# A gated mix of a state-space convolution and a GLU on one core: table parameters prepared for four channel groups at once, sums formed in place, PSUM banks and merge weights changed

## The chip, the cores and the metric

The program runs on one core of one Trainium2 chip. The metric is the time of one execution on the device, in microseconds (us), as the median of several runs. TensorE (PE in the rows, its weight loads PEld), VectorE (DVE) and ScalarE (ACT) each run their own list of instructions in order; SyncE (SP) issues all the DMAs, in order too. GpSimd does next to nothing here.

## The reference

The input u has 2048 rows (positions) of 512 channels. Three things are computed from it in float32:

```
g = sigmoid((u * gate_w).sum(-1))                       # one number a row
# a: a state-space convolution for each channel d, 128 states n
dt = exp(log_dt);  P[d,n,l] = exp(dt * A * l)           # A = A_re + i A_im
K[d,l] = real(sum_n C[d,n] * P[d,n,l] * dt * B[d,n])
a = causal_convolution(u, K) + u * Dskip                # by FFT in the reference
# b: a gated linear unit, 512 -> 1792 -> 512
b = (sigmoid(u @ w_gate) * (u @ w_up)) @ w_down
out = g * a + (1 - g) * b
```

## The kernel before

**The GLU** is most of TensorE's work. The 2048 rows are handled in two halves of two blocks of 512 (`half`, `sb`), the 1792 hidden columns in 14 pieces of 128 (`f`). Each float32 operand is split into a rounded high part and the rest (`split`: a copy on ScalarE, a difference on VectorE), and a product is made of three matmuls. So `hidden` issues 2 x 12 matmuls of 512 columns for each (half, sb, f) into two PSUM banks named `gups` (gate and up); `post` then takes a sigmoid of the gate (`sg`, ScalarE), multiplies it into the up bank (VectorE), and splits the product into `h` (ScalarE, VectorE). `down` multiplies `h` by the down weights into a bank named `dps`: for each of 3 or 4 pieces f (`GROUPS`) and each of 4 slices of 128 rows it issues 3 matmuls per f, so that 9 or 12 matmuls make one dps group; `add` then adds the bank, times 1 - g, to the accumulator `acc` (the first group of a row tile by a copy on ScalarE, the others on VectorE). The two kinds of matmul have one form and follow one another without a change of mode.

**The convolution** works by tables and three stages of small Fourier transforms. For each of 16 groups of 32 channels, `bases` takes the parameters `prm` and dt into `pg` and `dt`, makes angles and magnitudes (`aa`, `tn`, `ex`, `ep`) with sines and exponentials on ScalarE, the weights `w` = dt B C in parts, and the multipliers `bz`; `tables` makes two tables `T` (five doublings) and `B` from them on VectorE; TensorE multiplies these in 128 small matmuls (`kps`). `first` transforms the result (`wps`) and stores it as `a_k`. `rows` and `urest` do the same for u (`ups`, stored as `a_u`) and compute the row gate g. `passes` then runs 16 steps for each of two column halves j: `s2u` and `s2k` transform, VectorE multiplies (`tt`) and combines (`y`), `ips` transforms back, and the result goes to memory (`b_s`). `finals` takes it back (`b_in`), makes the last transform (`fps`) and adds it, times g, to the accumulator: for the first eight row tiles that was stored as `acc0`, so it is read back as `al` and the sum goes through `o` to the output. `steps` makes dt itself from log_dt at the start, by some twenty very small VectorE instructions.

**The order of the work** is made at build time. Each of these functions is a strand that yields (engine, planned duration, what to issue, what it depends on). `Plan.run` takes again and again the strand whose instruction has the smallest key: its planned start, plus the strand's entry in `BIAS`, plus `CHANGE` times the price of a change of mode. Only the resulting order and the semaphores go to the chip; planned times don't. `PACE` holds back the row tiles, `EARLY` says how long ahead of its data a strand may claim a bank, `SLACK` adds to planned latencies. Buffers are `slots`, taken and freed in planned time. PSUM's eight banks are dealt out by `BANKS`: `gu` for gups, `dn` for dps, `xb` for all the small transforms.

Of the kernel before, what the change touches and what calls it, by code (L numbers as in the profile page):

```python
# [36 lines left out]
NG = 16  # L37
ANGLES = list(range(33)) + [64 << k for k in range(5)]
# [7 lines left out]
BANKS = dict(gu=3, dn=2, xb=3)  # L46


BIAS = dict(x=-0.32, w=-0.26, split=0.4, rows=-0.12, dn=0.37, urest=1.2, bases=0.15, tables=0.35, first=0.46,
            hidden=0.91, post=0.08, down=0.69, add=0.25, passes=0.18, step=0.38, finals=0.54, last=0.21, const=4.77)  # L50
CHANGE = dict(ACT=0.5, PE=0.5)

XLATE = 0
PACE = [11.7, 12.7]
SLACK = dict(dma=0, eng=0)
EARLY = 0.21
# [156 lines left out]
def body(ctx, tc, xp, xt, prm, ldt, dsk, gw, wgu, wdn, c_wu, c_wf, c_wk, c_ww, c_pw, out):  # L213
# [47 lines left out]
    def steps():  # L261
# [27 lines left out]


    BZ, WS, PG, EX, EP, TA, TB, T2, KST, KEV = (slots(kp, n, k, s) for n, k, s in (
        ("bz", 1, [P, 3, 5, 32]), ("w", 1, [P, 3, 2, 32]), ("pg", 1, [P, 6, 32]), ("ex", 1, [P, 32, 2, NA]), ("ep", 1, [P, 32, NP]),
        ("ta", 1, [P, 32, 2, 32]), ("tb", 1, [P, 32, 2, 64]), ("t2", 2, [P, 32 * NA]), ("kst", 1, [P, 8, 64]), ("kev", 1, [P, 32, 64])))
    base = [[Ev(), None] for _ in range(NG)]
    kdone = [Ev() for _ in range(NW)]
    kleft = [w // 64 for w in WIDTHS]

    def bases():

        yield E["dt"]  # L300
        yield E["pw"]
        for gi in range(NG):
            t0 = [E["dt"].t, E["pw"].t]
            pgs, = yield PG, 1
            pg = pgs.tile("pg")
            dt = kp.tile([P, 1, 32], F32, tag="dt", name="dt")
            ta = yield "SP", kb(96), lambda: S.dma_start(pg, prm[gi].rearrange("p (a b) -> p a b", a=6)), t0 + [pgs.t]
            tb = yield "SP", kb(16), lambda: S.dma_start(dt[:, 0], dts[gi:gi + 1].to_broadcast([P, 32])), t0 + [pgs.t]
            exs, = yield EX, 1
            eps, = yield EP, 1  # L310
            dg = dt.to_broadcast([P, 2, 32])
            aa = kp.tile([P, 2, 32], F32, tag="aa", name="aa")
            tn = kp.tile([P, 32], I32, tag="tn", name="tn")
            ex, ep = exs.tile("ex"), eps.tile("ep")
            f, cs = ex[:, :, 1], ex[:, :, 0]

            def first():
                V.tensor_tensor(aa, pg[:, 0:2], dg, op=OP.mult)
                V.tensor_scalar(aa[:, 1], aa[:, 1], 1 / (2 * math.pi), None, op0=OP.mult)
            t = yield "DVE", 2 * dve(64) + 0.15, first, [ta, tb]  # L320
            sh = [P, 32, NP]
# [57 lines left out]
    def tables():  # L379
        for gi in range(NG):  # L380
# [52 lines left out]
            plan.spawn(first(gi, j, p, bank, t), BIAS["first"])  # L433

    kevs = {}

# [503 lines left out]
```

## Time and profile before

| what | value |
|---|---|
| median of 3 runs | 711.7 us (703.93 to 712.25) |
| the profiled execution's own time | 707.2 us |
| its span, first to last instruction | 705.4 us |
| PE busy | 669.2 us (95%), 6176 matmuls |
| DVE busy | 563.4 us (80%), 1041 instructions |
| ACT busy | 372.7 us (53%), 593 instructions |
| DMA | 133.96 MB, mean 190 GB/s |
| granted TensorE clock, mean | 0.995 |

Busy is the share of the span in which an engine had an instruction under way. The own time of the execution is 1.8 us longer than its span. A row of the view of waits gives who waited, for whom, the idle time in total, how often, and the longest; "issue" there means that the engine stood idle with nothing to wait for that the profile shows. Rows of the timeline give the start, the length, the engine, the line and the tile written, and in brackets the idle time before it.

### The profile page before, as it was taken

The page shows a single profiled execution, that of the slowest core. Times are in us where ns is not written, and L with a number is a line of the kernel's source. Part 1 is how long each engine was busy: PE and PEld are TensorE (multiplying, and loading weights), DVE is VectorE, ACT ScalarE, POOL GpSimd, SP SyncE. Part 2 cuts the span into 40 slices and gives each one's busy share as a digit, 9 for nine tenths or more (in the row PEclk, how much of TensorE's full clock was granted, in tenths as well). Part 3 has the DMA queues.
Part 4 walks back from the last instruction along what each step waited for, and adds up shares of the span by engine and source line. Part 5 has one row for each costly group of instructions (what it writes and reads, how often), then busy time and mean ns, then how long its engine had stood idle before and what let it go on. Part 6 is the DMA issues. An engine that isn't in the chain of part 4 may idle for free.

```text
span 705.4 us, 15192 instructions
## 1 busy us (share of the span) xinstructions
PE 669.2 (95%) x6176; PEld 484.8 (69%) x6176; DVE 563.4 (80%) x1041; ACT 372.7 (53%) x593; POOL 0.2 (0%) x4
## 2 busy tenths in 40 slices
PE   3999999999999999798999899999999899999987
PEld 2778677777778878686777567676677566666653
DVE  6699999999999999898899799999889434444424
ACT  5859587666768283737658283736482122223110
POOL 0000000000000000000000000000000000000000
PEclk9999999999999999999999999999999999999999
DMA  6946676645655464436356453534667756855466
GB/s 217 352 118 221 219 263 193 237 151 195 218 162 187 154 213 170 137 138 214 103 174 203 164 186 121 187 120 129 217 193 234 217 176 220 281 167 179 136 208 225
DMA packets 81030, 133.96 MB, mean 190 GB/s; under 512 B 9536, under 2 KB 48832, under 8 KB 76352
## 3 DMA queue, kind: packets, MB, share of 16 engines
q1 hardware_dynamic: 80960, 132.99, 57.6%
q8 instruction: 49, 0.80, 0.4%
q14 instruction: 21, 0.17, 0.1%
HBM read 79.48 MB, written 53.48 MB: 188 GB/s over the span
## 4 chain that ended last, share of the span: by engine, by line
PE 70%; DMA 11%; DVE 9%; issue 3%; SPq 3%; ACT 3%; DVEq 0%
PE gups L792 31%; PE dps L842 18%; PE ips L611 4%; PE s2u L538 4%; PE kps L428 4%; DMA au<-a_u 4%; PE s2k L538 4%; DMA al<-acc 3%; PE ups L509 2%; PE wps L456 2%; SPq L645 1%; DMA u<-xp 1%; DMA b_in<-b_s 1%; PE fps L658 1%; DVE T L374 1%
## 5 line engine op out<-in xcount | busy, mean ns | idle before, releaser
L792 PE MATMUL gups<-x,gu 128*128 128x512 f32 x1344 | 330.8, 398 | 16.6 <-ACT gu L721 8.5
L792 PEld LDWEIGHTS gups<-x,gu 128*128 128x128 f32 x1344 | 250.3, 189 | 87.6 <-issue 18.9
L842 PE MATMUL dps<-dnw,h 128*128 128x512 f32 x672 | 172.1, 399 | 0.0
L842 PEld LDWEIGHTS dps<-dnw,h 128*128 128x128 f32 x672 | 122.1, 188 | 43.2 <-issue 16.1
L813 ACT ACTIVATE h<-gups 128x512 fp32r<-128x512 f32 x56 | 33.3, 595 | 58.9 <-DVE gups L809 58.5
L809 DVE TENSOR_TENSOR gups<-gups,sg 128x512 f32<-128x512 f32 x56 | 39.0, 696 | 25.6 <-PE gups L792 23.1
L589 DVE TENSOR_TENSOR tt<-s2k,uf 128x512 f32<-128x512 f32 x32 | 22.0, 688 | 44.3 <-PE s2k L538 43.9
L807 ACT ACTIVATE sg<-gups 128x512 f32<-128x512 f32 x56 | 33.4, 597 | 27.9 <-PE gups L792 27.6
L862 DVE SCALAR_TENSOR_TENSOR acc<-dps,omg,acc 128x512 f32<-128x512 f32 x48 | 35.9, 747 | 14.6 <-PE dps L842 14.4
L373 DVE TENSOR_TENSOR t<-T,bz 128x64 f32<-128x64 f32 (+4 forms) x80 | 46.1, 576 | 1.6
L375 DVE TENSOR_TENSOR T<-T,t 128x64 f32<-128x64 f32 (+4 forms) x80 | 46.4, 580 | 1.1
L618 ACT ACTIVATE ev<-ips 128x256 f32<-128x256 f32 x64 | 21.1, 379 | 47.6 <-PE ips L611 47.6
L374 DVE TENSOR_TENSOR T<-T,bz 128x64 f32<-128x64 f32 (+4 forms) x80 | 46.1, 576 | 0.0
L468 ACT ACTIVATE kev<-wps 128x256 f32<-128x256 f32 x64 | 33.7, 666 | 19.1 <-PE wps L456 19.0
L578 ACT ACTIVATE uf<-s2u 128x512 f32<-128x512 f32 x32 | 19.1, 596 | 44.7 <-PE s2u L538 34.9
L814 DVE TENSOR_TENSOR h<-gups,h 128x512 fp32r<-128x512 f32 x56 | 38.4, 686 | 3.8 <-ACT h L813 3.3
L428 PEld LDWEIGHTS kps<-B,T 128*32 128x32 f32 x2048 | 29.7, 110 | 12.4 <-issue 9.7
L404 DVE TENSOR_TENSOR B<-ep 128x1024 f32<-128x1024 f32 x32 | 38.0, 1217 | 0.0
L428 PE MATMUL kps<-B,T 128*32 128x64 f32 x2048 | 32.5, 220 | 5.7 <-issue 3.1
L538 PE MATMUL s2u<-au,ww 128*64 128x256 f32 x256 | 34.7, 391 | 3.2 <-DMA au<-a_u 2.7
L611 PE MATMUL ips<-y,ww 64*128 64x256 f32 x256 | 37.1, 402 | 0.0
L538 PE MATMUL s2k<-ak,ww 128*64 128x256 f32 x256 | 34.2, 387 | 0.1
(79 smaller groups left out, 701.4 us busy)
## 6 DMA issues: line engine op xcount, KB each, us to landing
wsp<-gu SPq DMA_DIRECT2D x14, 1024.0 KB, 5.0
gu<-wsp SPq DMA_DIRECT2D x14, 1024.0 KB, 5.1
a_u<-evu SPq DMA_DIRECT2D x32, 256.0 KB, 3.6
a_k<-kev SPq DMA_DIRECT2D x8, 1024.0 KB, 5.1
ww<-c_ww SPq DMA_DIRECT2D x32, 256.0 KB, 2.8
au<-a_u SPq DMA_DIRECT2D x32, 256.0 KB, 4.1
ak<-a_k SPq DMA_DIRECT2D x32, 256.0 KB, 4.4
b_s<-ev SPq DMA_DIRECT2D x32, 256.0 KB, 4.3
```

The costliest lines, as they stand in the source:

```text
L373: yield "DVE", dve(n), lambda: V.tensor_tensor(t2, src, sb, op=OP.mult), [t, slot.t]
L374: t = yield "DVE", dve(n), lambda: V.tensor_tensor(dst, src, br, op=OP.mult), [t]
L375: t = yield "DVE", dve(n), lambda: V.tensor_tensor(dst, dst, t2[:, :, ::-1], op=OP.add), [t]
L404: tm = yield "DVE", dve(1024), lambda: V.tensor_tensor(B[:, d, 0].rearrange("p d (a b) -> p d a b", b=8), ep[:, d, 0:8, None].to_broadcast ...
L428: mm(p[32 * jj:32 * jj + 32, s], T[:, ch, c], B[:, ch, c], start=(c == 0), stop=(c == 1), tile_position=(0, 32 * jj), skip_group_check=True)
L538: mm(p[64 * kb_:64 * kb_ + 64, c], ww[:, kb_, 64 * c:64 * c + 64], a(kb_), start=True, stop=True, tile_position=(0, 64 * kb_), skip_group_ ...
L611: mm(pi[i], ww[r, 2 + c], y[r, c], start=(c == 0), stop=(c == 1), tile_position=(64 * i, 0))
L792: mm(p, gu[:, a, k, dc], x[:, b, dc], start=(dc + n == 0), stop=(dc == NC - 1 and n == 2))
L809: t = yield "DVE", dve(512), lambda: V.tensor_tensor(pu, pu, sg, op=OP.mult), [t, tu]
L814: t = yield "DVE", dve(512), lambda: V.tensor_tensor(h[:, 1], pu, h[:, 0].bitcast(F32), op=OP.subtract), [t]
L842: mm(p, h[:, a, 128 * s:128 * s + 128], dn[:, b], start=(f == f0 and n == 0), stop=(f == f0 + gn - 1 and n == 2))
L862: te = yield "DVE", dve(512) + 0.06, lambda: V.scalar_tensor_tensor(accs[t], p, omg[:, t:t + 1], accs[t], op0=OP.mult, op1=OP.add), [tp, b ...
```

## The change

1. **Parameters for four groups at once.** A new strand `preludes` loads `prm` and dt for 128 channels instead of 32 and computes from them, in wider instructions, the scaled A (`aa`, wrapped angle) and the finished product w = dt B C. They stand in one buffer `pp` that eight users (two for each of the four groups) free together. `bases` then only multiplies by the powers, and the start of `tables` takes w as it is: four small instructions in place of six, the first result written straight into `T`.
2. **Sums in place.** In `step`, the combination is written over its first operand in `tt`, and the buffer `y` is gone; `tt` is free only after `ips`. In `last`, the sum is written over `al`, `o` is gone, and there are three `al` buffers in place of two `al` and two `o`.
3. **One PSUM bank moves**: `gu` has four banks in place of three, `dn` one in place of two.
4. **New numbers in the merge**: BIAS, CHANGE, PACE, SLACK, EARLY, some planned durations; `first` claims its `kst` buffer earlier; `steps` has a bias of its own. The inputs are laid out for four groups.

```diff
-BANKS = dict(gu=3, dn=2, xb=3)
+BANKS = dict(gu=4, dn=1, xb=3)
...
+CHANGE = dict(ACT=1, PE=1.5)
+PACE = [36.1, 13.2]
+SLACK = dict(dma=0.23, eng=0.04)
+EARLY = 2.43
...
+    def preludes():
+        yield E["dt"]
+        for k in range(NG // NQ):
+            pgs, = yield PG, 1
...
+            def turns():
+                V.tensor_tensor(aa, pg[:, 0:2], dg, op=OP.mult)
+                V.tensor_tensor(pg[:, 2:4], pg[:, 2:4], dg, op=OP.mult)
+                V.tensor_scalar(aa[:, 1], aa[:, 1], 1 / (2 * math.pi), None, op0=OP.mult)
...
+            t = yield "ACT", act(QW), lambda: A.activation(tn, aa[:, 1], AF.Copy), [t]
+            def rest():
+                for c in range(2):
+                    V.tensor_tensor(pg[:, c], pg[:, 2 + c], pg[:, 4 + c], op=OP.mult)
+                for c in range(2):
+                    V.tensor_tensor(pg[:, 2 + c], pg[:, 2 + c], pg[:, 5 - c], op=OP.mult)
+                V.tensor_tensor(aa[:, 1], aa[:, 1], tn, op=OP.subtract)
+                V.tensor_tensor(w[:, 0], pg[:, 0], pg[:, 1], op=OP.subtract)
+                V.tensor_tensor(w[:, 1], pg[:, 2], pg[:, 3], op=OP.add)
...
             def start():
-                V.tensor_tensor(w[:, 2, 0], w[:, 0, 0], w[:, 1, 1], op=OP.subtract)
-                V.tensor_tensor(w[:, 2, 1], w[:, 0, 1], w[:, 1, 0], op=OP.add)
-                V.tensor_tensor(w[:, 0], w[:, 2], ex[:, None, :, 0, 32].to_broadcast([P, 2, 32]), op=OP.mult)
-                V.tensor_tensor(w[:, 1], w[:, 2], ex[:, None, :, 1, 32].to_broadcast([P, 2, 32]), op=OP.mult)
-                V.tensor_tensor(T[:, :, 0, 0], w[:, 0, 0], w[:, 1, 1], op=OP.add)
-                V.tensor_tensor(T[:, :, 1, 0], w[:, 0, 1], w[:, 1, 0], op=OP.subtract)
+                V.tensor_tensor(T[:, :, :, 0].rearrange("p d c -> p c d"), w, ex[:, None, :, 0, 32].to_broadcast([P, 2, 32]), op=OP.mult)
+                V.tensor_tensor(w, w, ex[:, None, :, 1, 32].to_broadcast([P, 2, 32]), op=OP.mult)
+                V.tensor_tensor(T[:, :, 0, 0], T[:, :, 0, 0], w[:, 1], op=OP.add)
+                V.tensor_tensor(T[:, :, 1, 0], T[:, :, 1, 0], w[:, 0], op=OP.subtract)
...
-            V.tensor_tensor(y[:, 0], tt[:, 0, 0], tt[:, 0, 1], op=OP.subtract)
-            V.tensor_tensor(y[:, 1], tt[:, 1, 0], tt[:, 1, 1], op=OP.add)
+            V.tensor_tensor(tt[:, 0, 0], tt[:, 0, 0], tt[:, 0, 1], op=OP.subtract)
+            V.tensor_tensor(tt[:, 1, 0], tt[:, 1, 0], tt[:, 1, 1], op=OP.add)
...
-                    o, ph[i], g[:, t:t + 1], al, op0=OP.mult, op1=OP.add), [tp, ta, os_.t]
+                    al, ph[i], g[:, t:t + 1], al, op0=OP.mult, op1=OP.add), [tp, ta]
```

**What it moves at the start.** SyncE's list opens as follows before (`xt` is u transposed, staged as `st`; `ldt` is log_dt; `c_pw` the powers; `wgu` the gate and up weights; `dts` is dt going to memory).

```order
L717 DMA st<-xt 128x512 x4
L265 DMA steps<-ldt 16x32
L258 DMA pw<-c_pw 128x59
L717 DMA st<-wgu 128x512 x2
L717 DMA st<-xt 128x512
L717 DMA st<-wgu 128x512
L717 DMA st<-xt 128x512 x2
L288 DMA dts<-steps 16x32
```

And as follows now.

```order
L267 DMA steps<-ldt 16x32
L732 DMA st<-xt 128x512 x4
L260 DMA pw<-c_pw 128x59
L732 DMA st<-wgu 128x512 x2
L732 DMA st<-xt 128x512
L732 DMA st<-wgu 128x512
L290 DMA dts<-steps 16x32
L732 DMA st<-xt 128x512 x3
```

The load of log_dt has moved from behind four loads of u to the head, and the store of dt ahead of the two loads of u that it followed. On VectorE, all of `steps` now stands ahead of the first four differences of x; before, two of these stood ahead of it.

**What it moves in the down projection.** In the first half, near the eighth of the sixteen `kps`, TensorE's list reads before (the numbers tell the banks' uses and the h and weight tiles apart):

```order
L792 MATMUL gups_3317<-x_2849,gu_3086 128x512 x6
L842 MATMUL dps_3338<-dnw_2649,h_3038 128x512 x3
L842 MATMUL dps_3338<-dnw_2652,h_3089 128x512 x3
L842 MATMUL dps_3338<-dnw_2662,h_3284 128x512 x3
L842 MATMUL dps_3360<-dnw_2649,h_3038 128x512 x3
L842 MATMUL dps_3360<-dnw_2652,h_3089 128x512 x3
L842 MATMUL dps_3360<-dnw_2662,h_3284 128x512 x3
L842 MATMUL dps_3376<-dnw_2671,h_3329 128x512 x3
L792 MATMUL gups_3317<-x_2849,gu_3086 128x512 x6
```

And at the same point now:

```order
L855 MATMUL dps_2988<-dnw_2669,h_2913 128x512 x3
L805 MATMUL gups_2983<-x_134,gu_2192 128x512 x6
L855 MATMUL dps_3024<-dnw_2652,h_2611 128x512 x3
L855 MATMUL dps_3024<-dnw_2661,h_2736 128x512 x3
L855 MATMUL dps_3024<-dnw_2669,h_2913 128x512 x3
L805 MATMUL gups_3019<-x_134,gu_2320 128x512 x6
L855 MATMUL dps_3049<-dnw_2652,h_2959 128x512 x3
L855 MATMUL dps_3049<-dnw_2661,h_3032 128x512 x3
L805 MATMUL gups_3019<-x_134,gu_2320 128x512 x6
```

Before, whole dps groups follow one another, each into the other bank; now six gups matmuls stand between the end of one group and the start of the next, as there is only one bank. In the whole list, 37 of the 63 passages from one dps group to the next had no other work in between before. Now 3 have none, 4 have one small transform, 15 have just six gups matmuls, and the other 41 have more.

More of the change, by code (lines that the diff above doesn't have):

```diff
@@ L37 @@
 NG = 16
+NQ = 4
+QW = 32 * NQ
 ANGLES = list(range(33)) + [64 << k for k in range(5)]
@@ L45 @@
 WIDTHS = [256, 256]
-BANKS = dict(gu=3, dn=2, xb=3)
-BIAS = dict(x=-0.32, w=-0.26, split=0.4, rows=-0.12, dn=0.37, urest=1.2, bases=0.15, tables=0.35, first=0.46,
-            hidden=0.91, post=0.08, down=0.69, add=0.25, passes=0.18, step=0.38, finals=0.54, last=0.21, const=4.77)
-CHANGE = dict(ACT=0.5, PE=0.5)
+BANKS = dict(gu=4, dn=1, xb=3)
+BIAS = dict(x=-0.54, w=-0.09, split=0.5, rows=-0.19, dn=2.08, urest=1.21, bases=0.16, tables=0.35, first=0.3,
+            hidden=0.75, post=0.19, down=0.44, add=0.29, passes=0.14, step=0.27, finals=0.41, last=0.16, const=2.59, steps=-0.9, preludes=-0.12)
+CHANGE = dict(ACT=1, PE=1.5)
 XLATE = 0
-PACE = [11.7, 12.7]
-SLACK = dict(dma=0, eng=0)
-EARLY = 0.21
+PACE = [36.1, 13.2]
+SLACK = dict(dma=0.23, eng=0.04)
+EARLY = 2.43
 def constants():
@@ L293, in body @@
         ("ta", 1, [P, 32, 2, 32]), ("tb", 1, [P, 32, 2, 64]), ("t2", 2, [P, 32 * NA]), ("kst", 1, [P, 8, 64]), ("kev", 1, [P, 32, 64])))
     base = [[Ev(), None] for _ in range(NG)]
+    pready = [[Ev(), None] for _ in range(NG // NQ)]
     kdone = [Ev() for _ in range(NW)]
     kleft = [w // 64 for w in WIDTHS]
+    def preludes():
+        yield E["dt"]
+        for k in range(NG // NQ):
+            pgs, = yield PG, 1
+            pg = pgs.tile("pg")
+            dt = kp.tile([P, 1, QW], F32, tag="dt", name="dt")
+            tn = dt[:, 0].bitcast(I32)
+            src = dts.rearrange("(k g) d -> k (g d)", k=NG // NQ)[k:k + 1]
+            tb = yield "SP", kb(2 * QW // 4), lambda: S.dma_start(dt[:, 0], src.to_broadcast([P, QW])), [E["dt"].t, pgs.t]
+            ta = yield "SP", kb(3 * QW), lambda: S.dma_start(pg, prm[k].rearrange("p (a b) -> p a b", a=6)), [pgs.t]
+            pps, = yield PP, 1
+            pp = pps.tile("pp")
+            aa, w = pp[:, 0], pp[:, 1]
+            dg = dt.to_broadcast([P, 2, QW])
+            def turns():
+                V.tensor_tensor(aa, pg[:, 0:2], dg, op=OP.mult)
+                V.tensor_tensor(pg[:, 2:4], pg[:, 2:4], dg, op=OP.mult)
+                V.tensor_scalar(aa[:, 1], aa[:, 1], 1 / (2 * math.pi), None, op0=OP.mult)
+            t = yield "DVE", 2 * dve(2 * QW) + dve(QW) + 0.1, turns, [ta, tb, pps.t]
+            t = yield "ACT", act(QW), lambda: A.activation(tn, aa[:, 1], AF.Copy), [t]
[7 more added lines that the diff above has]
+                V.tensor_tensor(w[:, 1], pg[:, 2], pg[:, 3], op=OP.add)
+            t = yield "DVE", 7 * dve(QW) + 0.1, rest, [t]
+            pgs.free(t)
+            left[pps] = 2 * NQ
+            pready[k][1] = pp, pps
+            pready[k][0].set(t)
@@ L298, in bases, with used @@
+    def used(slot, t):
+        left[slot] -= 1
+        if left[slot] == 0:
+            del left[slot]
+            slot.free(t)
     def bases():
-        yield E["dt"]
         yield E["pw"]
         for gi in range(NG):
[L303 to L308, printed above, removed]
+            yield pready[gi // NQ][0]
+            pp, pps = pready[gi // NQ][1]
+            d = slice(32 * (gi % NQ), 32 * (gi % NQ) + 32)
+            t0 = [pready[gi // NQ][0].t, E["pw"].t]
@@ L331, in bases @@
+            used(pps, te)
             yield near(t)
```

77 lines of the change are left out of this document (26 added, 51 removed).

## Prediction

> **What bounds the kernel now.** I read the page's head first, then the busy time of each engine by stage, then TensorE's own waits.
>
> ```profile
> span 705.4 us, 15192 instructions
> PE 669.2 (95%) x6176; PEld 484.8 (69%) x6176; DVE 563.4 (80%) x1041; ACT 372.7 (53%) x593; POOL 0.2 (0%) x4
> ```
>
> I cut the span where the work changes: steady matmuls begin (13.4), the first kps (67), shortly before the last kps (547), after the last ips (661). Columns are length, then busy time of PE, PEld, DVE, ACT, POOL.
>
> ```profile
> 0.00:13.40 13.40, 1.22 (x2) 0.50 (x2) 6.84 (x29) 7.58 (x11) 0.20 (x4) 1.00 0.58 201
> 13.40:67.00 53.60, 52.92 (x219) 40.74 (x219) 44.97 (x83) 40.21 (x58) 0.00 (x0) 1.00 0.71 247
> 67.00:547.00 480.00, 467.24 (x4859) 349.53 (x4860) 445.96 (x809) 293.95 (x457) 0.00 (x0) 1.00 0.55 180
> 547.00:661.00 114.00, 110.17 (x856) 71.00 (x856) 51.01 (x99) 26.77 (x60) 0.00 (x0) 1.00 0.64 203
> 661.00:705.40 44.40, 37.60 (x244) 23.04 (x242) 14.66 (x27) 4.25 (x8) 0.00 (x0) 0.97 0.61 196
> ```
>
> In the long stage of the tables (67 to 547) PE is busy 467.24 of 480 us and DVE 445.96. Both are near full, so the question is which of them makes the other wait. PE is idle for 12.8 us there, 0.7 us in the stage ahead, 3.8 and 6.8 us in the last two, and 12.2 us at the start. The view of PE's waits says on whom:
>
> ```profile
> PE gups L792 <- ACT gu L721: 8.5, 1, 8.5
> PE gups L792 <- DVE gu L722: 3.7, 1, 3.7
> PE gups L792 <- issue: 3.1, 1, 3.1
> PE kps L428 <- issue: 3.1, 2, 2.0
> PE s2u L538 <- DMA au<-a_u: 2.7, 5, 1.0
> PE wps L456 <- issue: 1.8, 1, 1.8
> PE kps L428 <- DVE o L671: 1.3, 1, 1.3
> PE gups L792 <- ACT sg L807: 1.2, 2, 0.7
> PE kps L428 <- DVE T L375: 1.2, 1, 1.2
> PE fps L658 <- DMA b_in<-b_s: 0.9, 1, 0.9
> ```
>
> The first two are the start. The three rows of "issue", 8.0 us together, lie in the table stage, in the middle of blocks of matmuls and without a semaphore to wait for; nothing in the change touches their cause as far as the profile shows it. That leaves 12.8 - 8.0 = 4.8 us in 480 in which PE waited for data. For the tables themselves it waited 1.2 us, once. So PE bounds this kernel, and DVE, though 93% busy, delivers almost always in time. The number of matmuls is unchanged; what can be won is idle time of PE.
>
> **The start.** Before the second pair of matmuls PE waits for the low half of the first weights:
>
> ```profile
> 0.73 1.81 SPq L717 DMA_DIRECT2D st<-xt  x4
> 2.59 0.43 SPq L265 DMA_DIRECT2D steps<-ldt  x1
> 4.17 1.26 ACT L721 ACTIVATE x<-st 128x512 fp32r<-128x512 f32 x2 [2.16 <-DMA st<-xt]
> 7.29 0.17 DVE L268 TENSOR_SCALAR steps<-steps 16x32 f32<-16x32 f32 x1 [1.13 <-DMA steps<-ldt]
> 11.54 1.27 DVE L722 TENSOR_TENSOR x<-st,x 128x512 fp32r<-128x512 f32 x2
> 12.74 1.27 DVE L722 TENSOR_TENSOR gu<-st,gu 128x512 fp32r<-128x512 f32 x2
> 13.47 9.37 PE L792 MATMUL gups<-x,gu 128*128 128x512 f32 x34 [3.70 <-DVE gu L722]
> ...
> dts<-steps SPq DMA_DIRECT2D x1, 2.0 KB, 1.3
> ```
>
> The small instructions of `steps` hold DVE from 7.29 to 11.54, 4.25 us, because their 2 KB arrived only 4.7 us after the issue at 2.59, behind four loads. Now that load is issued first, at 0.73. How fast it lands alone no row shows: 1.3 us is what the 2 KB store took, 4.7 us what this load took behind the others; the first load of u, issued at 0.73, was used at 4.17, that is after 3.4 us. I take 3.0, between the store and that row: steps from 3.75 to 8.0. Then come four x differences, at 1.27 us a pair less overlap (11.54 to 12.74, so 1.20), 2.4 us, to 10.4; then the first gu difference, 0.7 us (12.74 to 13.47): 11.1. Against 13.47 that is 2.4 us won. With 4.7 us it is 12.8 and 0.7 won; with 1.3 us it is 9.4 and 4.0 won, if ScalarE's rounded halves, whose loads all start 0.43 us later, aren't late in their turn. I take **-2.1**, a little under the middle value, for that 0.43.
>
> **Parameters for four groups.** On DVE:
>
> ```profile
> 0.00:705.40 705.40, 26.25 (x144) 1.00 0.58 190
> ...
> L318 DVE TENSOR_TENSOR aa<-pg,dt 128x64 f32<-128x64 f32 x16 | 3.5, 218 | 1.4 <-DMA dt<-dts 1.4
> L374 DVE TENSOR_TENSOR T<-T,bz 128x256 f32<-128x256 f32 x16 | 6.7, 418 | 0.0
> L374 DVE TENSOR_TENSOR T<-T,bz 128x128 f32<-128x128 f32 x16 | 4.6, 285 | 0.0
> L358 DVE TENSOR_TENSOR bz<-ex,ep 128x320 f32<-128x320 f32 x16 | 13.1, 819 | 8.6 <-ACT ep L353 8.6
> ```
>
> The first row is all that works on the tile `w`: nine instructions in each of 16 groups, 26.25 us. With it go three on `aa`, at most 218 ns each: 16 x 0.65 = 10.5. Removed: 36.7 us. Added: four of the nine stay in kind, 26.25 x 4/9 = 11.7; and four preludes of ten instructions, two of 256 columns (418 ns) and eight of 128 (285 ns): 4 x 3.1 = 12.5. DVE loses 36.7 - 11.7 - 12.5 = **12.5 us**, nearly all of it in the table stage. On ScalarE twelve short roundings and some table loads go; it was idle for 186 of those 480 us, so I cost that at nothing. On SP, 32 loads become 8.
>
> What of the 12.5 us lies on the path? Only what PE waited for: the 4.8 us at most, and not all of these are DVE's (au and u come by DMA). I take **-3.0**; ends 0 and -4.8. The rest is hidden under PE: DVE will be idle more. The prelude itself adds a wait: it needs `pp` to be freed by the fourth group's start, and its small ScalarE step stands in a queue of longer ones. Behind it on DVE wait the next group's angles; but these also wait for `ex`, held by six operations on B, so the prelude's 3.1 us falls into time that DVE spends on B. If that cover went, three tables would come 3 us later each; PE has gups and dps to do meanwhile.
>
> **Sums in place.** The combination in `tt` has the same instructions; `tt` is held until ips, so the next product on DVE must wait for it. In the new order an s2k comes ahead of the ips of the step before it at only three places, and DVE was idle for 63 of 114 us in the stage where most steps of the second half lie. Nothing. Three `al` for two `al` and two `o` cost at most a landing (2.4 us) on one of the last sums: 0 to +2.4, taken as 0, since no more than three are in flight in the order.
>
> **Banks and order.** A fourth gups bank should end both waits "gups <- ACT sg": 0.7 us of the 1.2 is counted in the table stage, the other **-0.5** is not. The first eight fps move from among the last kps to a place among gups matmuls; the rows "kps <- DVE o", 1.3, and "fps <- b_in", 0.9, came from there: **-1.6**; ends 0 and -3.8, all the idle time of that stage.
>
> The single dps bank costs. Between two groups PE must now wait until the bank has been added to `acc`. Two places of the timeline, one quiet, one among table work, and between them a row of the chain that ended last, which gives the pace of matmuls:
>
> ```profile
> 654.74 0.84 PE L842 MATMUL dps<-dnw,h 128*128 128x512 f32 x3
> 655.62 0.75 DVE L862 SCALAR_TENSOR_TENSOR acc<-dps,omg,acc 128x512 f32<-128x512 f32 x1 [0.28 <-PE dps L842]
> ...
> 315.71 6.80 PE gups L792 x30
> ...
> 267.17 1.22 DVE L410 SCALAR_TENSOR_TENSOR B<-B,ex 128x1024 f32<-128x1024 f32 x1
> 267.33 4.02 PE L792 MATMUL gups<-x,gu 128*128 128x512 f32 x17
> 268.31 0.74 DVE L862 SCALAR_TENSOR_TENSOR acc<-dps,omg,acc 128x512 f32<-128x512 f32 x1
> ```
>
> In the quiet place the group's last matmul ends at about 655.4 and the sum at 656.37: 0.95 us. In the other the group ends at 267.33 and the sum at 269.05, 1.72 us, because one B operation had just begun. Thirty matmuls pass in 6.80 us, 227 ns each, so six gups cover 1.36 us. By count: three passages without cover cost 0.95 each, 2.9; two of these and one behind a single fps (0.5 us short) lie at the very end, on the path. Of fifteen with 1.36 us, I let one in five meet the late case (0.4 us short): 1.2. Sum 4.6; the gain from four gups banks elsewhere takes some back, so I enter **+4.0**. Ends: 0, if the order places each sum well, and +12, if half of the 15 and the 23 with up to 3 us are late by half a us and the rest stands. The Trainium skill's Perfetto Trace Analysis, in the section Matmuls, says that independent groups should rotate through different PSUM banks so that emptying one overlaps the next; this part of the change goes against that for dps. Charged at 0.95 us to each of the 22 passages with 1.36 us of cover or less, that rule would make the term 20.9 and the time 720.9; the trace's 0.95 is under 1.36, so I charge it to those without cover alone.
>
> **The sum**, against the profiled execution's own time: 707.2 - 2.1 - 3.0 - 0.5 - 1.6 + 4.0 = **704.0 us**. The three runs shown lie from 3.3 below to 5.1 above that execution, median 711.7; I shift nothing for that.
>
> **Rivals.**
>
> *VectorE was the limit.* For it: 93% busy in the stage, with PE slack of only 4.8 us because both were placed to fit; a table that is ready earlier lets everything behind it move up. Then all 12.5 us come through: 707.2 - 2.1 - 12.5 - 0.5 - 1.6 = 690.5, before any cost of the bank. Against: PE had only those 4.8 us to give. That works only if some of PE's busy time is hidden waiting, which the rows cannot exclude, as a matmul's end is modelled. 0.16.
>
> *The single bank stalls PE: slower.* If sums usually land behind one more operation of B (1.22 us), they land 0.95 + 1.2 = 2.15 us after the group: 0.8 us short at 19 passages, 15.2, and 2.15 at three, 6.5. Then 707.2 - 7.2 + 21.7 = 721.7 (7.2 for the four gains). It decides where sums land more than about 1.4 us after the group. Against: DVE's load falls, and the order is made with the bank in it. 0.06.
>
> *Short pauses lower the clock.* One stretch of the trace shows what a pause can do:
>
> ```profile
> 280.00:300.00 20.00, 16.46 (x249) 13.26 (x248) 17.65 (x32) 15.75 (x22) 0.00 (x0) 1.00 0.46 163
> 380.00:400.00 20.00, 16.90 (x257) 12.04 (x256) 16.03 (x24) 9.40 (x16) 0.00 (x0) 0.91 0.65 207
> ```
>
> After PE's 3.1 us of "issue" in the second, the granted clock averaged 0.91, so 1.8 us of 20 were lost; the 3.5 us idle in the first, in shorter pieces, cost no clock. If each of the 22 tightest passages set it off: 704 + 22 x 1.8 = 743.6. Against: those pauses are under 1 us. 0.03. The Trainium skill's TensorE: Matmul & The Clock Gate, section "A second HAM failure mode: psum-queue depth-cycling", tells of a kernel whose pauses between matmul groups kept switching the clock; by that rule this rival is the outcome, and the first row speaks against it.
>
> **Chances.** My forecast 0.75, the rivals 0.16, 0.06 and 0.03. The range: at the low end 707.2 - 4.0 - 4.8 - 0.5 - 3.8 = 694.1 with no cost of the bank, drawn to 690 to hold the first rival; at the high end +12 for the bank and little won, 716. A difference under 2%, 14 us, is what a measurement of this kernel can hardly tell from none. So faster means below 693: the first rival and the fringe of mine, 0.18. Slower means above 721: 0.08. The rest, 0.74.
>
> **What would show it.** Right: the start of steady matmuls near 11.4 us; DVE's busy total near 551 and PE's near 669; "issue" rows on PE still of some 8 us; new rows "PE dps <- DVE acc" of 3 to 6 us in total, the largest at the very end. Wrong: the table stage, 480 us here, more than 10 us shorter at the same PE work, which is the first rival; dps rows over 15 us, the second; several stretches of granted clock under 0.95, the third. What would break the sum most easily is the "issue" time, which I hold constant without knowing its cause: if it goes or doubles, the time moves by 8 us either way.

## The result

The changed kernel runs in 688.6 us (median; 687.56 to 689.7), the kernel before beside it in 708.6: the ratio is 0.972, 95% interval 0.965 to 0.979. Twice more, beside other experiments, it gave 0.978 (0.972 to 0.985) and 0.975 (0.968 to 0.982); the median of all its twelve runs is 689.2 us, that of all 66 runs of the kernel before 708.3. So it is faster by some 19 us. Medians are over all runs of a kernel; the ratios leave out a few slow ones (713 to 2244 us). The forecast was 704.0, 690 to 716, with 0.18 on faster: wrong in the number, in the range by a little, and in the outcome that it held likeliest (no clear difference, 0.74).

### The profile page after: what moved, and what is told of

Same layout as the page of the kernel before. It is cut to its first block, busy times and chain, and to the rows that moved or that the text cites. A ratio compares the mean times of both kernels' runs of the same rounds, so it can differ in the third digit from the quotient of the medians.

```text
span 686.7 us, 15044 instructions
## 1 busy us (share of the span) xinstructions
PE 661.4 (96%) x6176; PEld 483.0 (70%) x6176; DVE 555.9 (81%) x953; ACT 365.4 (53%) x576; POOL 0.2 (0%) x4
## 4 chain that ended last, share of the span: by engine, by line
PE 87%; DMA 6%; DVE 4%; issue 1%; SPq 1%; DVEq 0%; ACT 0%
PE gups L805 43%; PE dps L855 22%; PE ips L629 5%; PE kps L451 4%; PE s2k L560 4%; PE s2u L560 4%; PE ups L531 2%; PE wps L478 2%; DMA au<-a_u 2%; PE fps L676 1%; DMA pg<-prm 1%; DMA ak<-a_k 1%; DMA al<-acc 1%; DMA dts<-steps 1%; DVE B L426 1%
## 5 line engine op out<-in xcount | busy, mean ns | idle before, releaser
L855 PE MATMUL dps<-dnw,h 128*128 128x512 f32 x672 | 177.6, 403 | 5.5 <-DVE acc L875 2.5
L822 DVE TENSOR_TENSOR gups<-gups,sg 128x512 f32<-128x512 f32 x56 | 38.9, 695 | 14.4 <-PE gups L805 12.2
L600 ACT ACTIVATE uf<-s2u 128x512 f32<-128x512 f32 x32 | 19.1, 598 | 39.5 <-PE s2u L560 26.5
L629 PE MATMUL ips<-tt,ww 64*128 64x256 f32 x256 | 36.3, 402 | 0.0
L369 ACT ACTIVATE af<-ex 128x1216 int32<-128x1216 f32 x16 | 19.6, 1223 | 30.5 <-DVE ex L360 30.5
```

Source lines behind the costliest of these rows:

```text
L629: mm(pi[i], ww[r, 2 + c], tt[r, c, 0], start=(c == 0), stop=(c == 1), tile_position=(64 * i, 0))
L822: t = yield "DVE", dve(512), lambda: V.tensor_tensor(pu, pu, sg, op=OP.mult), [t, tu]
L855: mm(p, h[:, a, 128 * s:128 * s + 128], dn[:, b], start=(f == f0 and n == 0), stop=(f == f0 + gn - 1 and n == 2))
```

## The profile after

The head of the page of the changed kernel, whose profiled execution took 688.44 us:

```profile
span 686.7 us, 15044 instructions
PE 661.4 (96%) x6176; PEld 483.0 (70%) x6176; DVE 555.9 (81%) x953; ACT 365.4 (53%) x576; POOL 0.2 (0%) x4
```

Busy times by stage, with the same cuts in the program as in the prediction: first steady matmuls, first kps, a little before the last kps, after the last ips.

```profile
0.00:9.60 9.60, 0.02 (x1) 0.02 (x1) 6.33 (x28) 4.47 (x7) 0.20 (x4) 1.00 0.68 241
9.60:63.10 53.50, 51.43 (x203) 39.54 (x203) 45.52 (x76) 41.48 (x59) 0.00 (x0) 0.97 0.72 261
63.10:528.00 464.90, 462.28 (x4912) 345.12 (x4912) 439.69 (x735) 287.61 (x442) 0.00 (x0) 1.00 0.58 188
528.00:642.00 114.00, 111.27 (x823) 75.22 (x821) 48.88 (x89) 27.68 (x62) 0.00 (x0) 1.00 0.58 187
642.00:686.70 44.70, 36.39 (x244) 23.09 (x242) 15.46 (x28) 4.14 (x8) 0.00 (x0) 0.96 0.62 195
```

The last two stages are as long as before (114.00 and 44.70 us, before 114.00 and 44.40). The stage ahead of the first kps begins 3.8 us earlier. The long stage of the tables shrank from 480.00 to 464.90 us, and most of the gain lies there. Its work is about the same: it holds 64 of the small fps matmuls more, 18 dps more and 29 gups fewer. PE's idle time in it fell from 12.8 us to 464.90 - 462.28 = 2.6 us, and its busy time by 467.24 - 462.28 = 5.0 us.

Over the whole span PE's idle time fell by 10.9 us (from 36.2 to 25.3) and its busy time by 7.8 us (from 669.2 to 661.4), with the same 6176 matmuls and the same mean granted clock, 0.995. So a part of the old busy time was not needed for the matmuls themselves. The fps show some of it: sixteen of them pass in 0.66 us where nothing holds them, and took 1.64 us at one place of the old order, here with the old row first:

```profile
688.98 1.64 PE L658 MATMUL fps<-b_in,wf 64*32 64x256 f32 x16 [0.64 <-DVE acc L678]
429.26 0.66 PE L676 MATMUL fps<-b_in,wf 64*32 64x256 f32 x16
```

All 256 of them were busy for 17.96 us and are now for 12.77. The rest of the 7.8 us isn't told apart, as the busy times of different tiles overlap and don't add up.

PE's waits say which idle time went:

```profile
PE gups L805 <- ACT gu L736: 9.6, 1, 9.6
PE dps L855 <- DVE acc L875: 2.5, 3, 0.8
PE wps L478 <- issue: 1.7, 2, 1.4
PE fps L676 <- issue: 1.6, 1, 1.6
PE s2u L560 <- DMA au<-a_u: 1.5, 4, 0.5
PE dps L855 <- DVE dnw L737: 1.3, 1, 1.3
PE dps L855 <- ACT dnw L736: 0.8, 1, 0.8
PE dps L855 <- ACT h L826: 0.6, 1, 0.6
PE s2u L560 <- ACT sg L820: 0.6, 1, 0.6
```

"Issue" was 8.0 us in three rows, all in the table stage. It is 3.3 us now, and of that the 1.6 ahead of an fps and 1.4 of the wps row lie after the last kps block has begun: under 1 us is left in the table stage (1.6 us in a later profile of the same kernel). The waits of kps for VectorE's results and of gups for sg are gone. The single dps bank shows the row that was forecast, at 2.5 us a little under the 3 to 6.

## What the pauses named "issue" are

Theory: TensorE waits there for its own instructions. The queue named "instruction" moved 49 packets, 0.80 MB, 16 KB each; with 12352 matmuls and weight loads, one packet is 256 instructions, a page. The 256 instructions of a kps block pass in 1.9 us. If a page comes late the engine stands, and where it stands depends on how the pages lie in the program. The rival: the pauses belong to the work around them.

**The kernel before once more**, unchanged:

> The kernel before, unchanged, profiled a second time. Theory F (instruction fetch): the pauses of TensorE put down to 'issue' in its waits (8.0 us in total in the first profile, at 291, 329, 391 and 490 us) are late fetches of 16 KB of its instructions where a kps block uses up 256 instructions in 1.9 us; they come back at the same places, 6 to 10 us in total, and a fetch on DMA queue 8 starts within 3 us before each pause ends. Theory C (chance): they lie elsewhere, or their total is under 4 us.

It took 713.5 us in its only execution, and the four pauses stood at the same places, 3.2, 1.8, and two of together 2.7 us. A packet of the instruction queue begins 2.25 to 2.37 us before each of them ends, as theory F had said.

**Half a page more.** Half of the first kps block is issued twice: 128 instructions that change no result, so that all later instructions lie half a page further along.

```diff
-            def small():
-                for s in range(8):
+            def small(ns=8):
+                for s in range(ns):
...
-            t = yield "PE", ("128x32", 1.83), small, [t, tb, bank.t]
+            t = yield "PE", ("128x32", 1.83), (lambda: (small(4), small())) if gi == 0 else small, [t, tb, bank.t]
```

> The kernel before, but half of the matmuls of the first kps block are issued twice (same result): 128 instructions and about 1.0 us of work more, so that every later matmul sits half a page of 256 instructions (16384 B, one packet of the instruction queue) further along; nothing else changes. Theory F (the mid-block 'issue' pauses of TensorE come from late instruction packets, and where they hit depends on how the pages lie in the program): the four pauses of 1.3 to 3.3 us near 290, 329, 391 and 490 us do not come back at the same matmuls; the 'issue' rows of the table stage change by more than 3 us, down towards 0 or up, and the time changes by as much plus 1.0: 701 to 707 if they vanish, above 713 if there are more. Rival N (they belong to the work around those places: the loads of parameters issued just before, or VectorE's and ScalarE's load): they stay at the same four kps blocks with 7 to 10 us together, and the time is 709.7, within 2.

702.3 us, ratio 0.9915 (0.988 to 0.995): 5.3 us faster with 1 us of work added, and "issue" in all fell from 8.0 to 2.7 us. **A whole page more** (`small(), small()` in the same place):

> The kernel before with all of the first kps block issued twice: 256 instructions, one whole page, and about 1.9 us of work more, so that every later matmul has its old place in its page again, only one page later; the order is the same. In the kernel with half a page more, the four pauses of the table stage had left their places and 6 us were won. Theory F (it is the place of a kps block in its pages that decides): the four pauses come back at the same kps, gups and wps blocks with 6 to 10 us together, and the time is 707.6 + 1.9 = 709.5, within 2. Rival T (any change of the times by a microsecond moves the pauses, their places are accidents of timing): they don't come back at these blocks, and the time is about 702 to 705.

709.8 us, ratio 1.0035 (1.000 to 1.007). TensorE's timeline at one wps block, in the kernel before, with half a page and with a whole page:

```profile
328.33 0.80 PE L456 MATMUL wps<-wk,kst 64*64 64x64 f32 x37
330.93 0.68 PE L456 MATMUL wps<-wk,kst 64*64 64x64 f32 x27 [1.80 <-issue]
```

```profile
326.92 1.16 PE L456 MATMUL wps<-wk,kst 64*64 64x64 f32 x64
```

```profile
328.95 0.80 PE L456 MATMUL wps<-wk,kst 64*64 64x64 f32 x37
331.83 0.82 PE L456 MATMUL wps<-wk,kst 64*64 64x64 f32 x27 [2.09 <-issue]
```

The block stops after its 37th matmul, passes in one piece with half a page more, and stops after its 37th again with a whole page. The longest pause behaves likewise; the kernel before, and then the one with a whole page more:

```profile
390.35 0.73 PE L792 MATMUL gups<-x,gu 128*128 128x512 f32 x2
394.18 4.19 PE L792 MATMUL gups<-x,gu 128*128 128x512 f32 x11 [3.09 <-issue]
```

```profile
394.97 0.73 PE L792 MATMUL gups<-x,gu 128*128 128x512 f32 x2
397.51 2.80 PE L792 MATMUL gups<-x,gu 128*128 128x512 f32 x11 [1.80 <-issue]
```

So these pauses hang on the place in the page, to a single matmul. The time met the theory's number (709.5). Not all of it held: of the other two pauses, at the kps blocks near 291 and 490 us, one did not come back and the other was 0.2 us. The place says where a pause can be; how long it gets depends on something else besides. The half page has a pause of its own at another kps block, 1.4 us near 416 us, and two under 0.8 us.

The traces of all 17 profiles say what else. Number TensorE's instructions in order: matmuls, weight loads and the waits for semaphores between them. Of 56 pauses named "issue", 46 end at an instruction whose number is 193 above a multiple of 256, in every kernel, and a packet of the instruction queue begins 2.2 to 3.0 us before each of these ends. In none of the 817 pages that can be counted so does the first instruction come less than 2.2 us after the start of its packet. So the start of the packet makes the pause. In the kernel before, the page ahead of the pause of 3.1 us passed in 4.50 us, but the next packet began only 5.68 us after TensorE had entered that page. Another page passed in 2.88 us and no pause followed, because the next packet had begun 2.49 us before TensorE entered it. Why a packet begins early or late isn't shown. This is the one packet of that queue, q8, between 391 and 394.2 us of the kernel before (packets, MB, share of the DMA engines' time):

```profile
q8 instruction: 1, 0.02, 1.8%
```

The other 10 pauses, nine of them ahead of an fps, end at other numbers, and no packet begins in the 5 us before. They have another cause, which stays open; the 1.6 us ahead of an fps in the changed kernel is one of them.

**The same half page in the changed kernel:**

> The changed kernel with the same half page of 128 more matmuls in the first kps block, about 1.0 us of work. Theory F: pauses of 1 to 3 us come back in the table stage at one to four places, and the time is 691 to 699. Rival N (the changed kernel has no such pauses because the work around its kps blocks is lighter): no pause over 1 us in the table stage, and 689.6, within 1.0.

Its profiled execution took 684.9 us, its median is 692.4 (684.86 to 693.49; ratio 0.975, 0.968 to 0.982). In the profile no pause over 1.1 us is left in the table stage: the two wps pauses are gone, one of 1.0 us at the first kps is new, the one of an fps near the end stayed at 1.3, at the same matmul although every page had moved. By its numbers theory F just holds (one pause of 1.0 us, 692.4 us), but that execution was the fastest of the four, and what the others lost isn't in its profile. The new order seems to have few places where a shift can hurt.

In the changed kernel the pause of the wps block behind the last kps stands at the same matmul in all three profiles; the first and the last:

```profile
534.62 0.68 PE L478 MATMUL wps<-wk,kst 64*64 64x64 f32 x27
536.65 0.80 PE L478 MATMUL wps<-wk,kst 64*64 64x64 f32 x37 [1.36 <-issue]
```

```profile
535.09 0.68 PE L478 MATMUL wps<-wk,kst 64*64 64x64 f32 x27
536.99 0.80 PE L478 MATMUL wps<-wk,kst 64*64 64x64 f32 x37 [1.23 <-issue]
```

What the place is worth: 707.6 - 702.3 + 1.0 of added work = 6.3 us between a bad place and a better one, in one and the same order (some 2.6 us either way, by the interval of the ratio).

## What VectorE's relief is worth

**Less work in the old order.** The kernel before with the product by C left out of the parameters (so C is missing from the result), 11.5 us of VectorE:

```diff
-                V.tensor_tensor(w[:, 0], w[:, 2], cb(0), op=OP.mult)
-                V.tensor_tensor(w[:, 1], w[:, 2], cb(1), op=OP.mult)
...
-                V.tensor_tensor(w[:, 2, 0], w[:, 0, 0], w[:, 1, 1], op=OP.subtract)
-                V.tensor_tensor(w[:, 2, 1], w[:, 0, 1], w[:, 1, 0], op=OP.add)
```

> The kernel before with TensorE's, ScalarE's and SyncE's order as it was, but without four small VectorE instructions in each of 16 groups: the products with C and their sum are left out, so w is dt times B. That takes 16 x 0.72 = 11.5 us from VectorE. Theory V (VectorE was the limit): 8 to 12 us faster, ratio 0.983 to 0.989. Theory P (TensorE bounds it, VectorE's load matters little): 0 to 4 us faster, ratio 0.994 to 1.000, with the 'issue' pauses of TensorE still there.

704.2 us, ratio 0.9919 (0.9885 to 0.9952): 4.6 us, just over theory P's 0 to 4. Three of the four pauses stayed, 1.6 to 3.0 us each; the fourth was gone, and "issue" in all was 1.7 us less, so about 3 us are left for VectorE. With the half page as well:

> The kernel before with the product by C left out of the parameters (11.5 us less on VectorE, C missing from the result) and the half page in the first kps block (1.0 us more on TensorE). If the two causes add: 702.3 (half a page alone) less 4.5 (the product left out alone, 708.8 to 704.2) = 697.8, within 1.5, with 'issue' rows of the table stage under 2 us. If the pauses gave VectorE its time to catch up, so that they hide one another: above 700. If without pauses all of VectorE's relief counts: below 694.

702.2 us against 706.9 of the kernel before beside it, ratio 0.9956 (0.992 to 1.000). That is no faster than the half page alone (0.9915): the two do not add. That the pauses had given VectorE time to catch up fits the number (above 700), but isn't shown. Where the pauses were gone, 11.5 us less of VectorE bought nothing that these runs can see.

**More work in the new order.** The product of the powers is formed twice in each group, or three times, with the same result: 12.3 or 24.6 us more.

```diff
-            te = yield "DVE", dve(32 * NP), lambda: V.tensor_tensor(
-                ep, pp[:, 0, 0, d, None].to_broadcast(sh), pw[:, None, NA:].to_broadcast(sh), op=OP.mult), t0 + [eps.t]
+            def powers():
+                for _ in range(2):
+                    V.tensor_tensor(ep, pp[:, 0, 0, d, None].to_broadcast(sh), pw[:, None, NA:].to_broadcast(sh), op=OP.mult)
+            te = yield "DVE", dve(32 * NP), powers, t0 + [eps.t]
```

> The changed kernel in the changed order, with one VectorE instruction of 672 columns issued twice in each of 16 groups (the same result is written again): 16 x 0.77 = 12.3 us of VectorE put back, what the preludes save. Against the kernel before: theory V: the gain shrinks by 8 to 12 us, ratio 0.984 to 0.990 in place of 0.972. Theory P: by 0 to 4 us, ratio 0.971 to 0.978.

694.1 us, ratio 0.980 (0.976 to 0.983): 5 us by the medians, 3 by the ratios, for 12.3.

> The changed kernel with the powers' product formed three times in each group: 24.6 us more on VectorE (580 in all), the order unchanged, nothing left out. With once more (12.3 us) it was 694.1 against 688.6 and 692.1 without. Theory P (VectorE is covered, 12 us are worth 2 to 5): 692 to 699. Theory V (VectorE is the limit of the table stage): 706 to 714, with 'kps <- DVE T' or 'dps <- DVE acc' over 12 us.

706.9 us, ratio 1.000 (0.996 to 1.003), 18.3 us above the changed kernel beside it. Theory P was wrong for this size. The second 12.3 us cost 13 us, two and a half to four times the first. PE's waits in it:

```profile
PE dps L857 <- DVE acc L877: 6.5, 7, 1.5
PE dps L857 <- DVE dnw L739: 2.9, 4, 1.2
PE kps L453 <- DVE T L401: 2.8, 6, 0.9
```

The time is theory V's, its sign is not: neither the row of T nor that of acc is over 12 us. Together the three rows are 12.2 us. So VectorE's cover for work at this place of the new order is some 12 us deep and no deeper. Before the cover ends, work on VectorE costs about a third of itself; behind it, all. And one reading bounds the term: the kernel with 12.3 us more has VectorE busy for 568.6 us, more than the 563.4 of the kernel before, and still runs at 694. At most 5 of the 19 us are VectorE's in the new order. In the old order it is 0 to 5.

## What the fourth gups bank is worth

The changed kernel with three gups banks and two dps banks again; its order is made anew with them.

```diff
-BANKS = dict(gu=4, dn=1, xb=3)
+BANKS = dict(gu=3, dn=2, xb=3)
```

> The changed kernel with three gups banks and two dps banks as before, all else as changed; the merge makes another order. If the single dps bank costs what its waits show (2.5 us in the view of TensorE's waits), and the fourth gups bank brings nothing, 2 to 4 us less than the changed kernel, ratio 0.966 to 0.970. If four gups banks are what ends TensorE's waits for data in the table stage (8.3 us before, 2.9 after), 3 to 8 us more, ratio 0.976 to 0.984. 'issue' pauses may come at other places in this order: 0 to 10 us, told apart in its waits.

695.9 us, ratio 0.983 (0.980 to 0.9855), 6.7 us above the changed kernel's 689.2 (3 to 8 us by its three ratios). The row that answers:

```profile
PE gups L805 <- ACT sg L820: 7.2, 6, 1.8
```

Six times PE waited for a gups bank that a sigmoid had still to read, 7.2 us; with four banks no gups waits for a sigmoid. The dps row, 2.5 us, is gone in exchange. As the order differs too, the two rows are a reading, not a proof that nothing else differs.

## The parts alone

The old kernel with only the new weights, the new structure and banks with the old weights, and the structure alone:

```diff
-BIAS = dict(x=-0.32, w=-0.26, split=0.4, ...)
-CHANGE = dict(ACT=0.5, PE=0.5)
+BIAS = dict(x=-0.54, w=-0.09, split=0.5, ...)
+CHANGE = dict(ACT=1, PE=1.5)
...
-PACE = [11.7, 12.7]
+PACE = [36.1, 13.2]
```

> The kernel before with nothing but the new weights in the merge (old parameters per group, old product, three gups banks and two dps banks). Theory O (most of the gain is another order, which happens to meet the instruction pages better and waits less): 695 to 701, with 'issue' rows of the table stage under 4 us. Theory S (the gain needs the changed structure: fewer VectorE instructions, worth 5.5 us, and the fourth gups bank, worth 7 us; weights were chosen for it and mean nothing without it): 706 to 714, 'issue' rows near 8 us.

> The changed kernel (parameters for four groups, sums in place, four gups banks and one dps bank) with the old weights in the merge. Theory O (the order from the new weights brings most): 699 to 706, 'issue' rows near 8 us or dps waits over 6 us. Theory S (structure and banks bring it): 687 to 693.

> The changed structure alone: parameters for four groups and sums in place, with the old weights and three gups banks, two dps banks. If the structure alone brings what its VectorE instructions are worth: 701 to 704. If the time hangs on how the order falls out more than on the structure, as with the old weights and the new banks (715): anywhere from 700 to 720, with 'issue' rows and the wait of fps for b_in as the two that make the difference. Of the two I hold the second likelier.

| structure | banks gu, dn | weights | median us | ratio, 95% interval |
|---|---|---|---|---|
| old | 3, 2 | old | 708.3 | 1 |
| old | 3, 2 | new | 726.8 | 1.026 (1.020 to 1.031) |
| new | 3, 2 | old | 731.3 | 1.035 (1.027 to 1.044) |
| new | 4, 1 | old | 715.1 | 1.0075 (1.003 to 1.012) |
| new | 3, 2 | new | 695.9 | 0.983 (0.980 to 0.986) |
| new | 4, 1 | new | 689.2 | 0.972 to 0.978 |

The banks alone, and the old structure with one dps bank, were not run. Each part that was run alone makes the kernel slower: the weights by 19 us, the structure by 24 against the old kernel's runs beside it, further out than the 720 that I had held possible. Together they win. Both theories, O and S, were wrong: neither the order from the new weights nor the structure brings the gain by itself. The new weights are worth 26 us with the new structure and banks, 35 with the new structure and the old banks, and cost 19 with the old structure. Where such an order loses can be seen in the timeline of the old kernel with new weights:

```profile
687.58 3.53 PE L658 MATMUL fps<-b_in,wf 64*32 64x256 f32 x16 [5.49 <-DMA b_in<-b_s]
...
694.37 1.10 PE L658 MATMUL fps<-b_in,wf 64*32 64x256 f32 x14 [2.02 <-DVE o L671]
698.47 1.60 PE L658 MATMUL fps<-b_in,wf 64*32 64x256 f32 x16 [3.00 <-DVE o L671]
```

All eight last fps of a half stand at the end, with nothing between them to cover their loads and sums. In the new structure with old weights, the largest single loss behind the start is a page that comes late four matmuls from the end of a kps block:

```profile
334.77 1.98 PE L451 MATMUL kps<-B,T 128*32 128x64 f32 x124
341.08 0.43 PE L451 MATMUL kps<-B,T 128*32 128x64 f32 x4 [4.32 <-issue]
```

and the granted clock was half behind it, as the stretch of the pause and the one after it show (the last three columns are the granted clock, the DMA share and GB/s):

```profile
337.00:341.00 4.00, 0.00 (x0) 0.00 (x0) 1.43 (x2) 1.01 (x2) 0.00 (x0) 0.75 1.03 348
341.00:345.00 4.00, 3.92 (x12) 3.00 (x13) 3.35 (x7) 0.82 (x2) 0.00 (x0) 0.50 0.14 37
```

The structure alone has 5.9 us of "issue" at three kps blocks and 10.7 us of fps waiting for the sums in `al`.

## What makes the changed kernel vary

> The changed kernel once more, unchanged, for its spread and for which of its pauses come again. Theory F: pauses that come from the place in the pages come again at the same blocks: 1.6 us at about 534 and 1.6 us at about 667 us, no others over 1 us; time 687 to 691. If pauses are accidents of timing: at other blocks.

692.1 us (688.79 to 696.41); its profiled execution was the slowest of them. The pauses came again at the same blocks, 1.2 us at the wps and 1.7 us at the fps, and no other over 1 us, as theory F had said; the time was a little over its 691. In that profile VectorE's rows, then TensorE's, ahead of one kps block:

```profile
446.58 1.22 DVE L398 TENSOR_TENSOR T<-T,bz 128x1024 f32<-128x1024 f32 x1
452.35 0.48 DVE L687 SCALAR_TENSOR_TENSOR al<-fps,g,al 128x256 f32<-128x256 f32 x1 [4.55 <-DMA al<-acc]
452.75 1.22 DVE L399 TENSOR_TENSOR T<-T,t 128x1024 f32<-128x1024 f32 x1
```

```profile
454.11 2.15 PE L451 MATMUL kps<-B,T 128*32 128x64 f32 x72 [3.58 <-DVE T L399]
```

A last sum of one of the eight early fps stands in VectorE's queue between two steps of the table. It waits 4.55 us for the load of `al`, the table's last step waits behind it, the kps block behind that, and then the clock is half (columns as in the stages above, the granted clock third from the end):

```profile
450.00:454.10 4.10, 0.53 (x3) 0.13 (x2) 1.75 (x3) 0.00 (x0) 0.00 (x0) 0.87 0.25 74
454.10:458.00 3.90, 3.89 (x129) 3.73 (x130) 3.00 (x6) 1.13 (x3) 0.00 (x0) 0.50 0.89 296
```

In the first profile of the changed kernel the same sum waited 1.08 us, and no kps waited:

```profile
447.15 0.49 DVE L687 SCALAR_TENSOR_TENSOR al<-fps,g,al 128x256 f32<-128x256 f32 x1 [1.08 <-DMA al<-acc]
```

To test it, four `al` buffers in place of three, beside the changed kernel again:

```diff
-                        ("ev", 2, [P, 2, W]), ("al", 3, [P, W])):
+                        ("ev", 2, [P, 2, W]), ("al", 4, [P, W])):
```

> The changed kernel, unchanged, as the reference of this batch: 687 to 693. If the wait of VectorE for the early loads of al decides its spread, a profiled execution under 690 shows under 2 us of wait for al<-acc ahead of the kps block at 445 to 455 us, one over 693 shows 3 us or more there and a stretch of granted clock near 0.5 behind it.

> The changed kernel with four al buffers in place of three, so that the load of the third early last sum is issued ahead of four b_in loads, not behind them; up to about 440 us the order is the same, behind that it falls out anew. Theory L (that load is what decides the spread): no wait of VectorE over 1.5 us for al<-acc ahead of a kps block, no 'kps <- DVE T' over 1 us, and a time within 2 us of the faster runs of the changed kernel, 686 to 690, with a spread under 4 us. Rival (the order behind 440 us decides more than that load): 690 to 705, by 'issue' rows or waits of fps at its new places.

The changed kernel gave 688.6 (687.18 to 689.61), with a wait of 0.67 us at that sum. With four buffers: 689.4 (687.5 to 690.85), ratio 0.976 (0.970 to 0.982), no such wait over 1.1 us, no kps waiting for T. That is within the numbers of theory L, but the kernel beside it was as even and as fast, so the buffer isn't shown to help; only that this wait explains most of the one slow profile. None of the runs gives a version that is clearly better than the changed kernel.

## Why the prediction was wrong, point by point

**"Issue", held constant at 8.0 us, is the first step that failed.** The text named it as what would break the sum most easily, with 8 us either way, and then gave it no chance of its own. In the table stage it fell from 8.0 to under 1 us. The half page shows that such a change is worth 6.3 us without any other change of order. The view that could have told more was at hand: the row of the instruction queue, and pauses that stop a block in its middle.

**PE's busy time, held at 669 us, is the second.** The prediction said that the number of matmuls is unchanged and that what can be won is idle time of PE. The busy time came out at 661.4: of the 18.7 us by which the span shrank, 7.8 are busy time and 10.9 idle time. The fps view has 5.2 us less. In the table stage it is 5.0 us less, and there the half clock behind the pause of 3.1 us, 1.8 us by the prediction's own reading, is a part. The rest stays open.

**The banks, charged +4.0 and credited -0.5.** The charge was about right in kind and size: 2.5 us at three places, 0.8 each; the other passages are covered, as argued. The rule of the Trainium skill's Perfetto Trace Analysis, section Matmuls, by which independent groups rotate through different banks, would have given 720.9 if each tight passage had to pay; the trace agrees with it only at the passages without cover. The credit was too small, as far as the run with three banks shows: I took the fourth gups bank to be worth the waits "gups <- sg" that the old order shows, 1.2 us. But the old order had been made around three banks. With the new weights three banks cost 6.7 us, in an order that is made anew for them. A wait that an order avoids is not seen in its trace.

**VectorE, -3.0 (0 to -4.8).** The saving itself was 563.4 - 555.9 = 7.5 us, not 12.5. I priced the four small instructions that stay at the average of nine, 11.7 us; they are the longer ones:

```profile
L414 DVE TENSOR_TENSOR T<-pp,ex 128x64 f32<-128x64 f32 x16 | 4.5, 279 | 7.0 <-PE kps L451 6.9
L415 DVE TENSOR_TENSOR pp<-pp,ex 128x64 f32<-128x64 f32 x16 | 4.4, 276 | 0.6
L416 DVE TENSOR_TENSOR T<-T,pp 128x32 f32<-128x32 f32 x16 | 3.5, 217 | 0.6
L417 DVE TENSOR_TENSOR T<-T,pp 128x32 f32<-128x32 f32 x16 | 3.3, 205 | 0.0
```

16 x 0.977 = 15.6 us, 3.9 more. (Of the other 1.1 us: the three instructions on `aa` were 3.5 + 2.9 + 2.9 = 9.3 us, not 10.5, which is 1.2 us less to remove; the preludes came out at 11.8 us, not 12.5; the 0.6 us left are within what VectorE's total varies by, 555.6 to 556.5 us in three profiles.) The worth on the path holds: 7.5 us at the 3 to 5 us that 12.3 cost are 2 to 3.

**The start, -2.1.** Steady matmuls begin at 9.58, not 11.4: 3.9 us earlier than before. Nothing of it is left at the first kps: 18 matmuls fewer lie ahead of it (203 in place of 221; the one that begins at 9.58 stands in two stages above), at the pace of the steady ones 18 x 0.227 = 4.1 us, and it comes 3.9 us earlier (the cuts ahead of it stand at 63.1 and 67.0). The first dps groups now wait for their weights, 0.8 and 1.3 us close together, and the clock falls after them (the same columns):

```profile
28.00:30.00 2.00, 2.00 (x6) 1.56 (x5) 0.33 (x1) 1.99 (x3) 0.00 (x0) 0.52 1.01 408
30.00:32.00 2.00, 2.00 (x7) 1.61 (x6) 0.00 (x0) 2.00 (x2) 0.00 (x0) 0.62 1.02 408
```

That is 2 x 0.48 + 2 x 0.38 = 1.7 us, with the 2.1 of waiting 3.8. I had asked what would be late after ScalarE's halves, and not what the down weights would do.

**The first eight fps, -1.6 (0 to -3.8).** The waits of kps for o and of fps for b_in are gone from the table stage, as forecast. The move has a price that I had put at 0 under the sums in place: their loads of `al` now stand in VectorE's queue among table work, and in one of the profiles cost some 6 us (3.6 of waiting, and half the clock for 3.9 us and a little more behind it).

**The rivals.** "VectorE was the limit" gave 690.5, nearly the measured time, and its sign in the profile, a table stage more than 10 us shorter, did appear, though not at the same PE work, and PE's busy time had something to give, as this rival needed. But VectorE's load is not what held PE up: the relief alone gave 4.6 and 0 us, and with VectorE busier than before the new order still runs at 694. A sign that several causes share shows none of them. "The single bank stalls PE" fell with the 2.5 us. "Short pauses lower the clock" has two places, not 22: the one above, at the start, and 669 to 675 us with a granted clock of 0.72, behind pauses of 0.6, 0.2 and 1.6 us within 4 us. Two waits for the single bank, 0.84 us each within 4 us, cost none: 1.00 from 675 to 680 us.

**The sum.** From 708.3 to 689.2 are 19.1 us. By the single runs: the pauses some 6, the moved bank 6.7, VectorE 2 to 3, the start 0; together 15 to 16. The rest is not told apart, and the table of parts warns against adding them: the same parts in other company lose 7 to 23 us. What the forecast lacked most is this: it priced the edits against an order that the change throws away.

## What to carry to other kernels

Where a change also re-makes the order of work, price the order first, with a wide range: here the order around one and the same structure moved the time by 26 us, and waits that the old order avoided cannot be read from its trace. Give every stall without a named cause a chance of going or doubling, and test it by shifting the program by half a page of instructions, which costs a microsecond. Test an engine's slack by adding work to it in two sizes: one size shows a price, two show where the cover ends.

## What the runs showed of the hardware

TensorE can wait for its own instructions: pauses of 1.1 to 4.3 us in the middle of a block, at the same matmul from run to run. Half a page of 128 instructions took all four of one kernel away, a whole page of 256 brought two of them back, and 46 of 56 pauses in 17 profiles end where a new page begins, 2.2 to 3.0 us after its packet began. The Trainium skill's Runtime: NRT & Kernel Launch, section Instruction fetch mechanics, says that instructions come in blocks of 256 and that the cost of crossing a block is mostly hidden. The trace agrees on the blocks (49 packets for some 12500 instructions). On the cost it agrees for most pages, 44 of the kernel before without a pause, but four pauses made 8.0 us there. Why a packet begins late at some places and not at others stays open: the pause of 4.3 us fell in a stretch where the DMA engines were fully busy, the 2.0 us near 292 us of the kernel before in one where from 291.2 to 293.4 us no packet began:

```profile
DMA packets 0, 0.00 MB, mean 0 GB/s; under 512 B 0, under 2 KB 0, under 8 KB 0
```

The clock fell to half after single pauses of 3.1, 3.6 and 4.3 us, and after two pauses of 0.8 and 1.3 us with 0.7 us of work between them, for some 3 to 6 us each time; after a single pause of 2.0 us it stayed at 1.00.
